# A down projection in 26 products on a 4 x 4 x 2 grid of blocks, where it had 28 from a 2 x 2 x 2 scheme

## The chip, the core and the metric

The kernel runs on one core of a Trainium2 chip. TensorE multiplies matrices from SBUF into PSUM, VectorE and ScalarE work on SBUF and PSUM, GpSimd (POOL in the profile) on SBUF, and SyncE (SP) issues most transfers between SBUF and the chip's memory (DRAM). Each engine takes its instructions in order and waits for others by semaphores. The metric is the device time of one execution in microseconds.

## The reference

A block of a network for 2048 tokens of width 576, all in float32:

```python
xn = layernorm(x)                        # 2048 x 576
s  = linear_attention(xn, wqkv) @ wo     # 32 heads, 2048 x 576
h  = gelu(xn @ w_gate) * (xn @ w_up)     # 2048 x 4608
return x + s * silu(h @ w_down)          # 2048 x 576
```

## The kernel before

**Stages.** The first 300 us make the layer norm, the linear attention and s, which is kept in DRAM (`s_d`). Then come 36 matrices (`matrix`, L713): for each of the 18 groups of 256 columns of F (`g`), one of w_gate and one of w_up. Then comes the down projection (`down_all`, L960).

**Two words.** A float32 operand of TensorE is cut in two fp32r words: the high word is a ScalarE copy, the low word is VectorE's difference (`split`, `cut`). A product of two such operands takes three passes (high x high, high x low, low x high) in down, and seven with the odd rows in gate and up (`PASSES`).

**Gate and up.** Each matrix is a 2 x 2 x 2 product in seven block products after Strassen and Winograd. X's blocks and their sums lie in SBUF as `X`; the weight's sums are formed by GpSimd (`mat_sums`, L666) in one tile, from a raw weight that one transfer brings (`load_mat`, L661). `matrix` runs the seven products one after another, each for two token halves `s` (14 matmuls of 512 columns, in the banks "al", "be", "ga", "de"), and after each one a step of other work from the list `todo[i]`: cutting the next matrix's weight, loading a weight. So a matrix is seven steps, and in this document a step is the time of one of these pieces. The function `done` gets a finished block of the result: for gate it is put through Gelu into a block of `hid`, for up it is multiplied into that block. `hid` are four tiles of two blocks of 128 x 512 each, new in each group.

**Sums of h.** Within an up matrix (`done` in `up_matrix`, L787), GpSimd forms four sums of h for each token half, and SyncE stores the seven forms of h that down wants (`hs_d`). Likewise each group's block of Wd is loaded (`load_down`), turned into four sums on GpSimd (`down_sums`) and stored (`td_d`).

**Down.** Again seven names of products (`PRODUCTS`), each over 18 groups, with two token halves of four token tiles: step `n` is one name and one group, 24 matmuls of 288 columns in eight banks (`down_mm`). The operands come back from DRAM: `load_s` loads h six steps ahead and `prep_s` cuts it three steps ahead into a ring of five; `load_t` loads Wd's form in chunks of four groups eight steps ahead, and `prep_t` cuts it three ahead. At the end of a name's last group, the eight banks are read into sums (`u`, `c22`, `yt`), and finished blocks of the output are closed (`close`): Silu on ScalarE, a product with s on VectorE, a sum with x on GpSimd, and a store. The last name's last four groups run token tile by token tile, so that closing overlaps (`close_last`).

**Order.** The program keeps each engine's order as it is written (`pin`). Tiles with the same tag share a buffer: a new one waits until all users of the old one are done. SBUF is full: 16 large buffers (`big`), three middle ones (`mid`), four `h` slots, six `gl` and four `tmp` tiles pass from stage to stage.

Of the kernel before, what the change touches and what calls it, by code (L numbers as in the profile page):

```python
# [46 lines left out]


# [4 lines left out]
def block_kernel(ctx, tc, x, xe, wq_d, wkv_d, wo, wgu_d, wd_d, out):  # L53
# [659 lines left out]
    def matrix(q, c22, done, todo):  # L713
# [40 lines left out]
    hid = {}  # L754

    def gate_matrix(g, todo):
        for s in SBS:
            for b in range(2):
                hid[s, b] = slot([P, 2, TBN], F32, f"h_{g}_{s}_{b}")

        def done(s, f, b, src):
            o = hid[s, b][:, f]
# [7 lines left out]
        matrix(2 * g, lambda s: hid[s, 1][:, 1], done, todo)  # L770
# [3 lines left out]
    H_AT = {"A11": 0, "A12": 1, "S1": 2, "A22": 3, "S3": 4, "S2": 5, "S4": 6}  # L774
    T_AT = {"T1": 0, "T3": 1, "T4": 2, "T2": 3}
    hs_d = [dr.tile([P, 2, 7, TBN], F32, name=f"hs_{g}") for g in range(NG)]
    td_d = dr.tile([NG, P, 4, HALF], F32, name="td")

    def up_matrix(g, todo):
        c22, sm = {}, {}  # L780
# [6 lines left out]
        def done(s, f, b, src):  # L787
            if src is None:
                src = c22[s]
            elif isinstance(src, tuple):  # L790
                o = src[0] if (f, b) == (1, 0) else tmp([P, TBN], f"u12_{g}_{s}")
                vec("tensor_add", o, *src)
                src = o
            h1, h2 = hid[s, 0], hid[s, 1]
            h = hid[s, b][:, f]
            vec("tensor_mul", h, h, src)
            d = hs_d[g][:, s]
            eng = nc.gpsimd if g == NG - 1 else nc.sync
            if (f, b) == (0, 1):
                sm[s] = [gl_tile([P, TBN], f"hs_{g}_{s}_{i}") for i in range(3)]  # L800
                pool("tensor_sub", sm[s][0], h1[:, 0], h2[:, 0])
                pool("tensor_add", h2[:, 0], h2[:, 0], h2[:, 1])
                pool("tensor_sub", sm[s][1], h2[:, 0], h1[:, 0])
                dma(out=d[:, 4], in_=sm[s][0], eng=eng)
                dma(out=d[:, 2:4], in_=h2, eng=eng)
            elif (f, b) == (1, 0):
                pool("tensor_sub", sm[s][2], h1[:, 1], sm[s][1])
                dma(out=d[:, 0:2], in_=h1, eng=eng)
                dma(out=d[:, 5], in_=sm[s][1], eng=eng)
                dma(out=d[:, 6], in_=sm[s][2], eng=eng)  # L810
# [3 lines left out]
    td = {}  # L814

    def load_down(g):
        td[g] = mid(1, [P, 4, HALF], F32, f"td_{g}")
        dma(out=td[g], in_=wd_d[g].rearrange("p f (c j) -> p (f c) j", c=2))

    def down_sums(g):  # L820

        r = td.pop(g)
        b11, b12, b21, b22 = (r[:, i] for i in range(4))
        pool("tensor_sub", b11, b12, b11)
        pool("tensor_sub", b12, b22, b12)
        pool("tensor_sub", b22, b22, b11)
        pool("tensor_sub", b21, b21, b22)
        dma(out=td_d[g], in_=r)

    PRODUCTS = (  # L830
        ("A11", "B11"), ("A12", "B21"), ("S2", "T2"), ("S1", "T1"),
        ("S4", "B22"), ("S3", "T3"), ("A22", "T4"),
    )
    CHUNKS = ((0, 4), (4, 8), (8, 12), (12, 16), (16, 18))
    T_RAW, T_RING, S_RING = (0, 9, 1), (13, 8, 10), (11, 7, 12, None, None)
    S_FIRST = {3: 3, 4: 5}
    N2 = len(PRODUCTS) * NG
    NC = len(PRODUCTS) * len(CHUNKS)
    tr, hr, tw, hw, made = {}, {}, {}, {}, {"t": 0, "tp": 0, "s": 0, "sp": 0}

    def load_t(upto):

        while made["t"] < min(upto, NC):
            n = made["t"]
            made["t"] += 1
            nm = PRODUCTS[n // len(CHUNKS)][1]
            g0, g1 = CHUNKS[n % len(CHUNKS)]
            r = big(T_RAW[n % len(T_RAW)], [P, 4, HALF], F32, f"tr_{n}")
            if nm in T_AT:
                src = td_d[g0:g1, :, T_AT[nm], :]  # L850
            else:
                f, c = int(nm[1]) - 1, int(nm[2]) - 1
                src = wd_d[g0:g1, :, f, c * HALF : (c + 1) * HALF]
            dma(out=r[:, 0 : g1 - g0], in_=src.rearrange("g p d -> p g d"))
            tr[n] = r

    def cut(hi, lo, src):
        act(hi, src, AF.Copy)
        vec("tensor_sub", lo, src, hi.bitcast(F32))

    def prep_t(upto):
        while made["tp"] < min(upto, NC):
            n = made["tp"]
            made["tp"] += 1
            g0, g1 = CHUNKS[n % len(CHUNKS)]
            o = big(T_RING[n % len(T_RING)], [P, 2, 4, HALF], F32R, f"t_{n}")
# [24 lines left out]
    def prep_s(upto):  # L891
        while made["sp"] < min(upto, N2):
# [3 lines left out]
            if at_:  # L896
                pr = big(at_, [P, 2, 2, TBN], F32R, f"s2_{n}")
# [388 lines left out]
```

## Time and profile before

| | |
|---|---|
| time, median of 3 runs | 1511.56 us (1511.38 to 1512.89) |
| span of the profiled execution, first to last instruction | 1509.8 us |
| first matmul of gate and up | 303 us |
| first matmul of down | 1102.6 us |
| last matmul of down | 1504.3 us |
| bytes moved by DMA | 257.33 MB |

Times in the profile are microseconds from the first instruction, unless marked ns. PE is TensorE's matmuls, PEld its weight loads, DVE VectorE, ACT ScalarE, POOL GpSimd, SP SyncE (SPq: its DMA issues). A group's row reads: line, engine, operation, written tile <- read tiles, shape out <- in, count | busy us, mean ns of one | idle us just before them, and what ended that idle time. A row of the timeline reads: start, length, engine, line, operation, tiles, count [idle before it <- what ended it]. A row of a stretch gives each engine's busy time with its count of instructions, TensorE's granted clock, the busy share of the 16 DMA engines and GB/s.

### The profile page before, as it was taken

The numbers are of one execution on the slowest core, as the hardware profiler recorded it, in microseconds if no ns is written. First come the engines' busy times: TensorE is split into PE (matmuls) and PEld (weight loads), VectorE is DVE, ScalarE is ACT, GpSimd is POOL, SyncE is SP. The second block draws the span as 40 slices with busy tenths as digits, with TensorE's granted clock in tenths as the row PEclk, the third lists the DMA queues.
The fourth block names the chain that finished last, engine by engine and source line by source line (L and its number), as shares of the span: only waits on it lengthen the run. The fifth ranks groups of instructions, "written<-read, shape, count | busy, mean of one in ns | idle before, by whom it ended". The sixth has DMA issues, their size and how long they took to land.

```text
span 1509.8 us, 22224 instructions
## 1 busy us (share of the span) xinstructions
PE 1497.4 (99%) x8344; PEld 1336.7 (89%) x8344; DVE 1068.7 (71%) x1567; ACT 555.4 (37%) x1008; POOL 545.2 (36%) x500
## 2 busy tenths in 40 slices
PE   8999999999999999999999999999999999999998
PEld 7989978988888888888888888888899999999998
DVE  7577466558878777887877788877785566565775
ACT  5434334433222332322223222232336454444443
POOL 4342241135555446555445655544440020000120
PEclk9999999999999999999999999999999999999999
DMA  4525004354433334434333443323678766787873
GB/s 170 181 102 205 5 2 172 141 220 171 160 146 134 116 129 171 171 143 162 110 127 143 171 171 135 151 106 134 213 273 308 236 203 232 240 273 232 295 248 114
DMA packets 112222, 257.33 MB, mean 170 GB/s; under 512 B 10146, under 2 KB 38690, under 8 KB 110066
## 3 DMA queue, kind: packets, MB, share of 16 engines
q1 hardware_dynamic: 110482, 247.00, 45.9%
q0 software_dynamic: 1632, 8.91, 1.6%
q8 instruction: 65, 1.06, 0.3%
q14 instruction: 43, 0.35, 0.1%
HBM read 157.93 MB, written 97.91 MB: 169 GB/s over the span
## 4 chain that ended last, share of the span: by engine, by line
PE 96%; DVE 2%; issue 0%; ACT 0%; DMA 0%; SPq 0%; POOL 0%; DVEq 0%; POOLq 0%; ACTq 0%
PE bd L913 26%; PE al L708 15%; PE de L708 15%; PE ga L708 15%; PE be L708 8%; PE kv L90 7%; PE q L90 4%; PE s L90 4%; PE kv_a L90 1%; PE xt L167 1%; PE d L90 1%; DVE s L87 0%; PE kw L90 0%; PE b L90 0%; DVE xo_B L87 0%
## 5 line engine op out<-in xcount | busy, mean ns | idle before, releaser
L913 PE MATMUL bd<-t,s 128*128 128x288 f32 x3024 | 401.4, 295 | 0.7 <-DVE s L87 0.7
L913 PEld LDWEIGHTS bd<-t,s 128*128 128x128 f32 x3024 | 401.0, 188 | 1.1 <-DVE s L87 0.9
L87 DVE TENSOR_TENSOR s<-sr,s 128x512 fp32r<-128x512 f32 x252 | 182.0, 762 | 117.9 <-ACT s L84 110.9
L84 ACT ACTIVATE s<-sr 128x512 fp32r<-128x512 f32 x252 | 149.0, 626 | 190.9 <-PE bd L913 126.0
L93 POOL TENSOR_TENSOR hs<-h,h 128x512 f32<-128x512 f32 x72 | 100.5, 1404 | 223.8 <-DVE h L87 220.9
L84 ACT ACTIVATE h<-h 128x512 f32<-128x512 f32 x108 | 67.1, 633 | 244.4 <-POOL sm L93 123.1
L93 POOL TENSOR_TENSOR sx<-sx 128x288 f32<-128x288 f32 x24 | 27.9, 1181 | 317.0 <-DVE sx L87 315.9
L90 PE MATMUL kv<-wkv,xo_B 128*128 128x384 f32 x672 | 125.5, 341 | 1.0 <-DVE pk L87 0.3
L90 PEld LDWEIGHTS kv<-wkv,xo_B 128*128 128x128 f32 x672 | 116.8, 189 | 2.7 <-POOL wkv L93 1.1
L87 DVE TENSOR_TENSOR wa<-raw,wa 128x256 fp32r<-128x256 f32 x72 | 80.5, 1119 | 52.1 <-ACT wa L84 46.8
L93 POOL TENSOR_TENSOR sm<-raw 128x384 f32<-128x384 f32 x72 | 75.9, 1054 | 110.4 <-DMA raw<-in_wgu_dram 71.7
L87 DVE TENSOR_TENSOR h<-h,u 128x512 f32<-128x512 f32 x108 | 97.0, 899 | 3.7
L84 ACT ACTIVATE wa<-sm 128x1152 fp32r<-128x1152 f32 x36 | 41.8, 1161 | 134.6 <-PE de L708 134.6
L87 DVE TENSOR_TENSOR wa<-sm,wa 128x768 fp32r<-128x768 f32 x72 | 64.9, 901 | 36.9 <-ACT wa L84 36.1
L93 POOL TENSOR_TENSOR td<-td 128x288 f32<-128x288 f32 x72 | 71.4, 992 | 50.0 <-DMA td<-in_wd_dram 45.8
L87 DVE TENSOR_TENSOR wb<-sm,wb 128x256 fp32r<-128x256 f32 x72 | 61.4, 852 | 20.6 <-ACT wb L84 20.0
L87 DVE TENSOR_TENSOR wb<-raw,wb 128x256 fp32r<-128x256 f32 (+1 forms) x108 | 70.3, 651 | 7.2 <-ACT wb L84 5.6
L84 ACT ACTIVATE u<-al 128x512 f32<-128x512 f32 x72 | 40.9, 593 | 88.3 <-PE al L708 88.3
L90 PE MATMUL q<-xo_B,wq 128*128 128x512 f32 x240 | 64.1, 395 | 0.0
L708 PE MATMUL al<-xo_B,wa 128*128 128x512 f32 x252 | 63.0, 389 | 0.0
L708 PE MATMUL al<-xr_B,wa 128*128 128x512 f32 x252 | 63.0, 389 | 0.0
L708 PE MATMUL be<-xo_T,wa 128*128 128x512 f32 x252 | 63.0, 389 | 0.0
(156 smaller groups left out, 2778.8 us busy)
## 6 DMA issues: line engine op xcount, KB each, us to landing
sr<-hs SPq DMA_DIRECT2D x252, 256.0 KB
hs<-h SPq DMA_DIRECT2D x68, 512.0 KB
raw<-in_wgu_dram SPq DMA_DIRECT2D x36, 768.0 KB
hs<-hs SPq DMA_DIRECT2D x102, 256.0 KB
td<-in_wd_dram SPq DMA_DIRECT2D x18, 576.0 KB
td<-td SPq DMA_DIRECT2D x18, 576.0 KB
tr<-td SPq DMA_DIRECT2D x16, 576.0 KB
tr<-in_wd_dram SPq DMA_DIRECT2D x12, 576.0 KB
```

What stands on the lines that cost most here:

```text
L84: pin(nc.scalar.activation(*args, **kw))
L87: pin(getattr(nc.vector, op)(*args, **kw))
L90: pin(nc.tensor.matmul(*args, **kw))
L93: pin(getattr(nc.gpsimd, op)(*args, **kw))
L167: pin(nc.tensor.transpose(xts[n][j][:, k, :], xs[:, j, k * P : (k + 1) * P], ident))
L708: nc.tensor.matmul(o, w[0:rows, wi, :], xop[0:rows, xi, :], start=(start and n == 0), stop=(n == len(PASSES) - 1), skip_group_check=True,)
L913: nc.tensor.matmul(banks[j][:, 0:HALF], hw[n, s][:, a, t * P : (t + 1) * P], w[:, c, g % 4], start=(new and g == 0 and m == 0), stop=(g == ...
```

## The change

The down projection becomes a product of 4 token blocks by 4 blocks of F by 2 halves of d in 26 block products (`PROD`), each over the nine pairs of groups ("macro blocks", `NM`). A macro block has 16 blocks of h (`var_of`: token block and F block), and 28 sums (`ADDS`: result, two operands, sign, and the step of 28 at which GpSimd forms it). 26 blocks and sums (`FORM`) are stored for down.

*In gate and up.* Blocks and sums of h live in 17 spots: the four `h` slots, the middle buffer 1 that Wd's block had, and the six `gl` tiles. A sum takes the place of an operand that nothing else wants, or the spot that came free first. A sum is formed in its step, stored a step later, and its spot counts as free a step after that. Sums of the last macro block run into down's first products. The results of up are summed in PSUM (into the banks "be", "ga", "de") where they went to SBUF, and multiplied into h from there. Wd's loads, sums and stores are gone from this stage.

*In down.* A product `p` is nine block products (`kt`) in five units (2, 2, 2, 2, 1), each of four token tiles and three passes, in four banks; two sets of banks alternate. The raw blocks of h of a unit are loaded (`load_unit`) once the same unit of the product before is through with its buffer, and cut two units ahead (`cut`); the low word takes the raw block's place. All nine macro blocks of a form of Wd lie in one large buffer (`reg`), eight buffers in all; a form is turned into the next one in place by VectorE (`CHANGES`, done in two halves, for product p + 1 while p runs), loaded anew where needed (`LOADS`, in thirds), and cut into two word buffers (`make_words`, in halves). After its last unit a product's banks are read into one or two of eight output sums (`read`, in the next product's unit 1); a sum's first read is a ScalarE copy, others are VectorE adds or subtractions. A finished output is closed per token tile, in the next product's units 2 to 4, with a store for each tile.

```diff
+ADDS = (
+    (18, 5, 13, 1, 13), (38, 12, 13, 1, 15), (20, 4, 8, -1, 15), (16, 5, 9, -1, 16),
...
+    (42, 17, 37, -1, 34), (29, 2, 10, 1, 34), (26, 10, 17, 1, 36), (30, 20, 26, -1, 36),
+)
+PROD = (
+    (24, 1, 0, ((5, 1), (7, 1))), (18, 1, 0, ((1, 1),)), (14, 0, 1, ((3, 1),)),
...
+    (4, 0, 0, ((4, 1), (6, -1))), (13, 1, 0, ()), (12, 0, 0, ((2, -1),)), (20, 0, 1, ((0, 1),)),
+)
         for s in SBS:
-            vec("tensor_add", c22(s), c22(s), bs["de", s])
-            done(s, 1, 1, None)
+            o = c22(s) if q % 2 == 0 else bs["be", s]
+            vec("tensor_add", o, c22(s), bs["de", s])
+            done(s, 1, 1, o)
...
+    def put_out(m, v, at):
+        eng = nc.gpsimd if m == NM - 1 else nc.sync
+        dma(out=hs_d[m][:, FORM.index(v)], in_=value(m, v), eng=eng)
+        used(m, v, at + 1)
...
+    def add_up(m, v, a, b, sign, at):
+        into = next((x for x in (a, b) if left[m, x] == 1), None)
+        va, vb = value(m, a), value(m, b)
+        born(m, v, None if into is None else place_of[m, into])
+        pool("tensor_add" if sign > 0 else "tensor_sub", value(m, v), va, vb)
...
         def done(s, f, b, src):
-            if src is None:
-                src = c22[s]
-            elif isinstance(src, tuple):
-                o = src[0] if (f, b) == (1, 0) else tmp([P, TBN], f"u12_{g}_{s}")
-                vec("tensor_add", o, *src)
-                src = o
...
+            if isinstance(src, tuple):
+                vec("tensor_add", src[1], *src)
+                src = src[1]
+            v = var_of(g, s, f, b)
+            h = value(m, v)
             vec("tensor_mul", h, h, src)
...
+            if v in FORM:
+                put_later(m, v, 7 * (2 * g + 1) + DONE[f, b])
...
+    UNITS = ((0, 2), (2, 4), (4, 6), (6, 8), (8, 9))
+    REG = {"22": 0, "42": 7, "32": 9, "12": 8, "31": 10, "41": 12, "11": 15, "21": 14}
...
+    def load_unit(p, k):
+        if p >= NP:
+            return
+        raw_v[p, k] = v = raw_place(p, k)
+        for i in range(*UNITS[k]):
+            dma(out=v[:, i - UNITS[k][0]].bitcast(F32), in_=hs_d[i][:, PROD[p][0]])
...
+    def cut(u):
+        p, k = divmod(u, NU)
+        if p >= NP:
+            return
+        hi, lo = hi_place(p, k), raw_v[p, k]
+        hi_v[p, k] = hi
+        src = lo.bitcast(F32)
         act(hi, src, AF.Copy)
         vec("tensor_sub", lo, src, hi.bitcast(F32))
...
+    CHANGES = {
+        4: (("12", "12", "-", "22"),), 5: (("41", "31", "-", "41"), ("32", "41", "+", "32")),
...
+        21: (("21", "21", "-", "32"),), 25: (("11", "11", "-", "31"), ("11", "11", "+", "41")),
+    }
...
+    def change(p, c):
+        for nm, a, op, b in CHANGES.get(p, ()):
+            r = [reg[x][:, HALVES[c]] for x in (nm, a, b)]
+            vec("tensor_add" if op == "+" else "tensor_sub", *r)
...
+    def read(p, js=range(TT)):
+        for o, d in PROD[p][3]:
+            a = acc_of(o)
+            for j in js:
+                src = banks[p % 2][j][:, 0:HALF]
+                if (o, j) not in begun:
+                    begun.add((o, j))
+                    act(a[:, j], src, AF.Copy)
                 else:
...
+                    vec("tensor_add" if d > 0 else "tensor_sub", a[:, j], a[:, j], src)
...
+    def close(o, j):
+        _, cols, rows = places(o)
+        y, t = acc_of(o)[:, j], sxs[o][j]
+        act(y, y, AF.Silu, scale=float(SIGN[o]))
+        vec("tensor_mul", t[:, 0], y, t[:, 0])
+        pool("tensor_add", t[:, 0], t[:, 0], t[:, 1])
+        dma(out=out[rows(j), cols], in_=t[:, 0])
...
+        for u in range(NP * NU):
+            p, k = divmod(u, NU)
+            n = KT * p + 2 * k
+            for at in sorted(events):
+                if at <= H_END + n // 2:
+                    run_events(at)
+            if p in LOADS and k < 3:
+                load_reg(*LOADS[p], k)
+            if k == 0:
+                for o, e in ENDS.items():
+                    if e == p:
+                        load_sx(o)
+            if k < 2:
+                change(p + 1, k)
+            elif k < 4:
+                make_words(p + 1, k - 2)
+            cut(u + 2)
+            if p == last and k == 2:
                 break
...
+            for kt in range(*UNITS[k]):
+                down_mm(p, kt, range(TT))
+            load_unit(p + 1, k)
+            if k == 1 and p:
+                read(p - 1)
+                late += [
+                    lambda o=o, j=j: close(o, j) for o, e in ENDS.items() if e == p - 1
+                    for j in range(TT)
                 ]
+            elif k > 1:
+                run(late, 3)
```

More of the change, by code (lines that the diff above doesn't have):

```diff
@@ new lines, in take_spot, with var_of, value, born @@
+    def take_spot():
+        i = min(free, key=lambda j: (free[j], j))
+        free.pop(i)
+        return i
+    def var_of(g, s, f, b):
+        return TP.index(2 * s + b) * 4 + KP.index(2 * (g % 2) + f)
+    def value(m, v):
+        return spots[place_of[m, v]]
+    def born(m, v, i=None):
+        place_of[m, v] = take_spot() if i is None else i
+        left[m, v] = sum((v == a) + (v == b) for _, a, b, _, _ in ADDS) + FORM.count(v)
+    def used(m, v, at, keep=False):
+        left[m, v] -= 1
+        if left[m, v] == 0 and not keep:
+            free[place_of[m, v]] = at
@@ L768, in done @@
             act(o, src, AF.Gelu_apprx_tanh)
[L770 to L777, printed above, removed]
+        matrix(2 * g, lambda s: h_of(s, 1, 1), done, todo)
     def up_matrix(g, todo):
-        c22, sm = {}, {}
+        c22 = {}
+        m = g // 2
         def take(s):
@@ L812, in up_matrix @@
-        matrix(2 * g + 1, take, done, todo)
[L814 to L850, printed above, removed]
-            else:
[L852 to L855, printed above, removed]
```

351 lines of the change are left out of this document (188 added, 163 removed), and 23 rows, old and new, of tables (ADDS, CHANGES, FROM, LOADS).

## The prediction

> **What bounds the kernel now.** I read the page first, then the chain of waits in order of time, then the stretches.
>
> ```profile
> span 1509.8 us, 22224 instructions
> PE 1497.4 (99%) x8344; PEld 1336.7 (89%) x8344; DVE 1068.7 (71%) x1567; ACT 555.4 (37%) x1008; POOL 545.2 (36%) x500
> PEclk9999999999999999999999999999999999999999
> ```
>
> TensorE is busy for 99% of the span at full granted clock. The chain of waits says the same by stage:
>
> ```profile
> 303.05 3.20 PE al L708 x14
> ...
> 1104.91 4.16 DVE s L87 x2
> 1113.20 391.44 PE bd L913 x2950
> ```
>
> From 303 us on the chain is TensorE alone, but for 4.16 us of VectorE where the down projection begins. So only fewer matmuls can gain, and only a new wait of TensorE can lose. How much room the other engines have is read from stretches of the two stages:
>
> ```profile
> core 0: us, PE busy (x) PEld busy (x) DVE busy (x) ACT busy (x) POOL busy (x), PEclk, DMA share, GB/s
> 700.00:800.00 100.00, 100.00 (x443) 82.78 (x442) 81.23 (x104) 27.29 (x46) 58.33 (x48) 1.00 0.43 158
> ...
> 1135.00:1140.00 5.00, 5.00 (x40) 5.00 (x39) 4.32 (x8) 3.61 (x7) 0.00 (x0) 1.00 1.05 387
> ...
> 1200.00:1300.00 100.00, 100.00 (x757) 100.00 (x756) 62.19 (x88) 49.49 (x80) 9.16 (x8) 1.00 0.67 225
> 1300.00:1400.00 100.00, 100.00 (x757) 100.00 (x756) 57.55 (x88) 47.73 (x79) 5.18 (x5) 1.00 0.72 234
> ```
>
> In gate and up VectorE is 81% busy and GpSimd 58%; in down VectorE is about 60% busy, GpSimd almost idle, and the DMA queues have shown 387 GB/s when full.
>
> **What the change is worth on TensorE.** Before, 7 names x 2 token halves x 18 groups of F are 252 block products (28 nines) of 4 token tiles x 3 passes, 3024 matmuls; now 26 products x 9 macro blocks are 234, 2808 matmuls. The chain gives 391.44 / 2950 = 132.7 ns for each. 216 fewer x 132.7 ns = **-28.7 us**. Shape and passes stay, so the price stays.
>
> **Gate and up: costed at nothing.** Here are the rows.
>
> ```profile
> L93 POOL TENSOR_TENSOR hs<-h,h 128x512 f32<-128x512 f32 x72 | 100.5, 1404 | 223.8 <-DVE h L87 220.9
> L87 DVE TENSOR_TENSOR h<-h,u 128x512 f32<-128x512 f32 x108 | 97.0, 899 | 3.7
> L93 POOL TENSOR_TENSOR td<-td 128x288 f32<-128x288 f32 x72 | 71.4, 992 | 50.0 <-DMA td<-in_wd_dram 45.8
> L87 DVE TENSOR_TENSOR h<-h,al 128x512 f32<-128x512 f32 x36 | 23.2, 685 | 0.5
> ...
> 702.75 1.75 PE L708 MATMUL al<-xo_B,wa 128*128 128x512 f32 x7
> ...
> 723.39 20.17 SPq L96 DMA_DIRECT2D raw<-in_wgu_dram  x2
> ...
> 726.51 1.29 DVE L87 TENSOR_TENSOR h<-u,de 128x512 f32<-128x512 f32 x2
> ```
>
> Per macro block (four matrices, 28 steps of one chain piece, 3.17 us each, 88.8 us) GpSimd did 16 sums of h at 1.40 and 8 of Wd at 0.99; now 28 of h and none of Wd: +16.8 - 7.9 = +8.9 us, from 58% to about 68% busy. VectorE's 108 products h<-h,u now read PSUM and should cost 685 ns like h<-h,al instead of 899: 108 x 0.214 = 23 us less work. An add that writes PSUM has no row; I take the 685 of one that reads it (bounds 685 and 899, 108 of them: 0 to 23 us of VectorE, covered by its 19% idle). Gone too are the loads and stores of Wd's sums on SyncE. Holding the "be" bank until the product with h is no wait: it is wanted by the second product of the next matrix, four products or 12.7 us after the one whose sum it takes.
>
> The tight place is the 17 spots. By the list of sums, the tightest block goes out at step 4, and its spot is rewritten at step 6. Its store stands on SyncE's queue behind the weight load of that step, which waits for its buffer: for the matrix that begins at 702.75 it goes at 723.39, 20.6 us in. The store then lands 2.3 to 4.9 us later (rows below), and VectorE wants the spot at 726.51, 23.8 us in. That is a wait of up to 2 us on VectorE once per macro block, hidden by the PSUM banks: what it delays is wanted three products (9.5 us) later. If that cover is gone, a step is lost per macro block (rival 3).
>
> **The middle of down: VectorE.** Now the prices for the new down stage.
>
> ```profile
> L87 DVE TENSOR_TENSOR xo_T<-xf_B,xo_T 128x1024 fp32r<-128x1024 f32 x8 | 9.8, 1226 | 12.4 <-ACT xo_T L84 12.4
> L87 DVE TENSOR_TENSOR s<-sr,s x37: 677/687/1301, 1200.0 to 1257.8; 128x512 fp32r<-128x512 f32 x37
> L87 DVE TENSOR_TENSOR u_d<-u_d,bd 128x288 f32<-128x288 f32 x15 | 6.4, 454 | 10.2 <-PE bd L913 10.2
> L87 DVE TENSOR_TENSOR sx<-y,sx 128x288 f32<-128x288 f32 x16 | 6.5, 448 | 0.0
> ```
>
> 1024 columns cost 1226 ns and 512 cost 687, so 1.05 ns a column: 1440 columns (five blocks of Wd) 1.66 us, 1152 (four) 1.36, both halves 3.03. A product of 108 matmuls lasts 14.33 us. In it VectorE has: low words of h, 4 x 1.226 + 0.687 = 5.59; low words of Wd, 3.03 (24 of the 26); a change of Wd in place, 3.03 each (20 of them); each read of the four banks into a sum, 4 x 0.454 = 1.82 (23, the first 8 go to ScalarE); four closing products 1.79 (8 outputs). Sum over the stage: 145 + 73 + 61 + 42 + 14 = **335 us of 372.6**, 90%, where it was 60%. The changes of Wd are the new item: GpSimd formed such sums before, in gate and up.
>
> To this comes GpSimd's interference:
>
> ```profile
> 1254.01 1.29 DVE L87 TENSOR_TENSOR s<-sr,s 128x512 fp32r<-128x512 f32 x2 [1.20 <-ACT s L84]
> ...
> 1228.77 2.11 POOL L93 TENSOR_TENSOR sx<-sx 128x288 f32<-128x288 f32 x2 [1.05 <-issue]
> 1228.92 2.50 DVE L87 TENSOR_TENSOR s<-sr,s 128x512 fp32r<-128x512 f32 x2
> ...
> 1104.91 4.16 DVE L87 TENSOR_TENSOR s<-sr,s 128x512 fp32r<-128x512 f32 x2
> 1105.52 1.30 POOL L93 TENSOR_TENSOR hs<-h,h 128x512 f32<-128x512 f32 x1
> 1106.89 1.62 POOL L93 TENSOR_TENSOR h<-h 128x512 f32<-128x512 f32 x1
> ```
>
> Two subtractions take 1.29 us alone and 2.50 beside two 288-wide GpSimd sums: 0.60 per sum. Beside two 512-wide sums they take 4.16: 1.43 per sum. The Trainium skill (SBUF — State Buffer, Who interferes with whom) says that a VectorE instruction with two SBUF inputs contends with GpSimd's reads, and calls the shared port pair "an exclusive lock". By that a 288-wide sum would cost its whole length (2.11 / 2 = 1.05) and not 0.60; the 512-wide rows agree with the rule, the 288-wide do not. By the rule the closings would cost 32 x 0.45 = 14 us more of VectorE, and the sum below would be 1511. I go by the row.
>
> An output's four closing sums thus add 2.4 us. Per product, excess over 14.33: while the 11th runs (15.3 + 2.4) +3.4 and the next (two changes, 16.5) +2.2, together 5.6; the 15th (17.1 + 2.4) +5.2; the 20th and 21st +1.0 and +3.4 = 4.4; the 24th and 25th (15.8 + 4.8; 14.7) +6.3 and +0.4 = 6.7. Lone products with two changes, +2.2, is below the slack. How much can be late unseen? A unit's h is cut two units (6.4 us) ahead; high words, low words and a unit's other work take some 4 of these; 2.5 us of slack remain. It can't grow: the raw buffer is refilled only after its own matmuls, so VectorE can't run ahead in the light products. Stalls: 3.1 + 2.7 + 1.9 + 4.2 = **+12 us**. Bounds: 3, since instructions in a row cost less (1.29 for two, not 1.37, some 40 ns x 370 = 15 us over the stage, about 9 of them where the excess stands); 21, with whole-length sums (4.9 + 4.5 + 3.7 + 7.8).
>
> ScalarE and SyncE stay under this, by these rows:
>
> ```profile
> L84 ACT ACTIVATE s<-sr 128x512 fp32r<-128x512 f32 x252 | 149.0, 626 | 190.9 <-PE bd L913 126.0 <-DMA sr<-hs 49.4 <-DVE sx L87 5.2
> L84 ACT ACTIVATE t<-tr 128x1152 fp32r<-128x1152 f32 x28 | 32.3, 1152 | 3.8 <-DMA tr<-in_wd_dram 3.8
> L96 SPq DMA_DIRECT2D sr<-hs x252: 319/390/1770, 1078.7 to 1477.6; - x126
> SPq L96 <- POOL sx L93: 30.0, 6, 6.7
> ```
>
> ScalarE's high words are 4 x 1.05 + 0.63 + 2.7 = 7.5 us of 14.33, with first reads or closings up to 11. SyncE issues 9 loads of h and up to 15 others at 0.39. Each closing's store now follows its own sum, 32 stores for 8, and waits for GpSimd; three in a row take some 4.5 us, and the loads of h behind them are asked for 12.7 us ahead and need 4.9 to land and 1.9 to be cut: hidden.
>
> **The start of down.** The last macro block's sums fall due after the last matrix.
>
> ```profile
> hs<-hs POOLq DMA_DIRECT2D x6, 256.0 KB, 5.7
> ...
> L96 POOL DMA_DIRECT2D hs<-hs x6: 539/546/584, 1104.4 to 1117.0; - x6
> ...
> DMA to landing us min/median/max: 2.3/4.9/6.6
> ```
>
> GpSimd has 18 sums left there, with stores that it issues itself at 0.55 each; 4.9 us is the median landing. Port: 14 of them fall in the first two products, 14 x 1.43 = 20 us, beside 5.6 + 8.6 us of VectorE and 3 of the last matrix (four adds at 0.69): 37 in 28.7. Of the 8 us over, 2.5 are slack, and GpSimd itself pauses for two landings, so I take 4 late. Order: up to the one that the third product's last unit needs there are 13 sums and 14 stores, 13 x 1.40 + 14 x 0.55 = 26 us, and two sums wait for the landing of a store that frees their spot (4.9 each): 36; that store lands at 41, the unit after it and its cut take 4.9 + 1.9 more, and TensorE wants it at 28.7 + 12.7 = 41.4. That would be 6 late; as part of the landing overlaps, I take 3. SyncE queues that load behind the store, and the next product's loads stand behind it. DMA bytes: the first product has 12 blocks of h to load and 8 to store at 0.26 MB and two forms of Wd at 1.33, 7.9 MB; the second 9, 8 and one, 5.8 MB. At 387 GB/s that is 20.4 and 15.0 us for 14.3 each: 7 us behind, just covered by loads asked for 12.7 us ahead. Together **+7 us** (0, if gaps between sums absorb it, as the 4.16 us before cost TensorE little; to 14, if none overlaps).
>
> **Sum.** 1511.6 - 28.7 + 0 + 12 + 7 = **1502 us**. The profiled execution's span is 1509.8; the runs are 1.8 us longer, and the same is added after: a span near 1500.
>
> **The rivals.** *1: the full gain.* VectorE's excess is absorbed: 3 us in the middle, 0 at the start: 1511.6 - 28.7 + 3 = 1486. For it: runs of instructions are shorter than single ones. Against: 90% of one in-order engine with two units of lead.
>
> *2: VectorE becomes the pace of down.* Whole-length sums (21), 14 at the start, and 1 us for each of four products with two changes, because a change stands ahead of the cuts in the queue: 1511.6 - 28.7 + 21 + 14 + 4 = 1522; it is a loss from the point where these stalls pass 28.7. For it: 335 + 32 x 1.05 = 369 of 372.6. Against: the 0.60 of the rows. The skill's exclusive lock, named above, is this rival's rule.
>
> *3: a spot's wait reaches TensorE in gate and up.* A step of 3.17 us in each of 9 macro blocks is 28.5: 1502 + 28.5 = 1531. For it: a lead of one step. Against: 9.5 us of cover and 19% idle VectorE.
>
> **How the numbers follow.** Forecast 0.50 (1494 to 1514 alone), full gain 0.17, VectorE 0.24, spots 0.09. This measurement can tell 0.2%, 3 us. Faster: all of the full gain and 0.40 of the forecast: 0.57. Within 0.2%: 0.08 of the forecast's upper end and 0.03 of milder forms of rival 2: 0.11. Slower: the rest, 0.32. The range runs from the full gain to about the middle of the two slow rivals, which leaves out less than 0.2: 1485 to 1522.
>
> **What would show it.** After: 2808 matmuls bd at 132.7 ns. VectorE about 90% busy in down, with stalls of 1 to 4 us that end on its cuts of h, near the 11th, 15th and 24th products and in the first three. Gate and up: TensorE 100% busy, no gap. h times up at about 685 ns. It is wrong if gaps stand before al, be, ga or de; if the stalls are ended by DMA; or if VectorE stays under 80% in down.

## The result, and the profile after

The changed kernel takes 1518.61 us (median of 4 runs, 1516.15 to 1521.74), the kernel before 1511.47 beside it: a ratio of 1.0047, 95% interval 1.0033 to 1.0061. It is 7 us slower, where some 10 us less were forecast. The profiled execution, on which all stages and stalls below rest, is the fastest of the four, 1516.15 us; the 2.5 us from there to the median are not in the account.

The page of the changed kernel:

```profile
span 1514.4 us, 21908 instructions
PE 1490.7 (98%) x8128; PEld 1314.1 (87%) x8128; DVE 1151.2 (76%) x1546; ACT 561.1 (37%) x923; POOL 635.9 (42%) x556
PEclk9999999999999999999999999999999999999999
```

TensorE lost only 6.7 us of busy time (1497.4 before), though 216 matmuls, 28.7 us, are gone. So the lost gain is not in gaps alone: part of the matmuls must take longer. Of the span's 4.6 us more, the stages hold (first matmul to first matmul): 1.9 us ahead of gate and up, **+14.3 us in gate and up** (799.7 to 814.0), and -11.5 us from the first matmul of down to the end (407.2 to 395.7). The stretches of gate and up and of down:

```profile
400.00:1100.00 700.00, 699.16 (x3034) 569.18 (x3034) 548.61 (x710) 197.44 (x325) 436.45 (x349) 1.00 0.33 112
1119.00:1508.00 389.00, 377.59 (x2804) 374.70 (x2803) 333.01 (x342) 195.26 (x237) 71.27 (x65) 0.99 0.79 255
```

and the first of them before:

```profile
400.00:1100.00 700.00, 700.00 (x3090) 579.63 (x3089) 550.78 (x726) 204.87 (x340) 365.25 (x310) 1.00 0.41 149
```

In the same 700 us of gate and up TensorE is busy throughout at clock 1.00 in both, and yet makes 3034 matmuls instead of 3090. A busy engine hides this: the count, not the busy share, shows it. Grouped by tiles, before (line, engine, operation, shapes, count, busy us, mean ns):

```profile
L708 PE MATMUL de<-xo_T,wa 128*128 128x512 f32 x224 | 56.0, 389 | 0.0
```

after, in the same stretch:

```profile
L737 PE MATMUL de<-xo_T,wa 128*128 128x512 f32 x217 | 55.6, 395 | 0.0
...
L737 PE MATMUL be<-xr_T,wa 128*128 128x512 f32 x217 | 54.2, 389 | 0.0
```

and TensorE in order of time, after (start, length of the seven matmuls):

```profile
716.04 1.75 PE L737 MATMUL be<-xr_T,wa 128*128 128x512 f32 x7
717.62 1.75 PE L737 MATMUL ga<-xo_T,wa 128*128 128x512 f32 x7
719.21 1.79 PE L737 MATMUL ga<-xr_T,wa 128*128 128x512 f32 x7
720.84 1.79 PE L737 MATMUL de<-xo_T,wa 128*128 128x512 f32 x7
722.47 1.79 PE L737 MATMUL de<-xr_T,wa 128*128 128x512 f32 x7
```

From start to start, the first two groups of seven take 1.58 and 1.59 us, the next ones 1.63: some 233 ns a matmul instead of 226.7. It is not a wait for VectorE, and not the matrix: with the same weights `wa`, in the same product `ga`, one token half is slow and the other is not. What differs between the halves is the buffer in which X lies.

In down the chain of waits shows where TensorE's own pieces are broken off, and what stands there in the longest other pieces:

```profile
1125.27 10.91 DMA raw_a<-hs
1139.70 12.29 PE bd L119 x79
1154.37 106.53 PE bd L119 x802
1261.38 5.31 DMA raw_h<-hs
1299.63 35.01 PE bd L119 x262
1344.15 124.08 PE bd L119 x933
1484.99 23.82 PE bd L119 x166
```

What TensorE waited for directly (us, times, longest us) is VectorE's cuts of h, at the start (`raw_a`) and later (`raw_h`, `raw_g`):

```profile
PE bd L119 <- DVE raw_h L116: 6.9, 5, 3.4
PE bd L119 <- DVE raw_a L116: 4.1, 3, 1.8
...
PE bd L119 <- DVE raw_g L116: 0.2, 1, 0.2
```

From here on a product's stall is the time from its first matmul to the next product's, less 108 times the undisturbed 132.7 ns. Products are counted from 0, as in the code; the prediction counted from 1. The stalls are 4.9 and 2.0 us in products 1 and 2 (the granted clock also fell to 0.89 from 1130 to 1145 us, so not all of the 4.9 is a gap), 2.1 in 11 and 12, 1.6 in 15, 0.1 in 21 and 7.0 in 24: 6.9 at the start and 10.8 later.

**The addresses.** The new tiles of Wd and of its words, `[P, 9, 288]`, have 10368 bytes a partition, the largest tiles of the kernel before, `[P, 5, 512]`, 10240. They share tags with the tiles of the earlier stages, so twelve of the sixteen large buffers grew by 128 bytes and every buffer laid out behind one moved. Before, all operands of gate and up start at a multiple of 256 bytes. After, by the addresses in the built program, `wa` starts at 128 modulo 256, `wb` at 0, and X's blocks thus (token half o, r):

| product | weights | X starts at | operands alike | seven matmuls each |
|---|---|---|---|---|
| al, be (B11, T2) | wa, 128 | 128, 128 | yes, yes | 1.58 to 1.62 us |
| ga (T1) | wa, 128 | 128, 0 | yes, no | 1.59, 1.63 |
| de (T3) | wa, 128 | 0, 0 | no, no | 1.63, 1.63 |
| al (B21) | wb, 0 | 0, 0 | yes, yes | 1.61, 1.59 |
| ga, de (B22, T4) | wb, 0 | 128, 128 | no, no | 1.62 to 1.64 |

Seven of a matrix's fourteen half products are unlike, and the first half product behind one is still a little slow. 7 x 0.045 us and 2 x 0.03 in each of 36 matrices make 13.5 us, near the 14.3. That is so far a fit, and no proof.

### The profile page after: what moved, and what is told of

Its sections match the earlier page's. It is cut to its first block, busy times and chain, and to the rows that moved or that the text cites. A ratio compares the mean times of both kernels' runs of the same rounds, so it can differ in the third digit from the quotient of the medians.

```text
span 1514.4 us, 21908 instructions
## 1 busy us (share of the span) xinstructions
PE 1490.7 (98%) x8128; PEld 1314.1 (87%) x8128; DVE 1151.2 (76%) x1546; ACT 561.1 (37%) x923; POOL 635.9 (42%) x556
## 3 DMA queue, kind: packets, MB, share of 16 engines
q8 instruction: 64, 1.05, 0.3%
## 4 chain that ended last, share of the span: by engine, by line
PE 92%; DVE 4%; DMA 1%; issue 1%; ACT 1%; POOL 0%; SPq 0%; DVEq 0%; ACTq 0%; POOLq 0%
PE bd L119 20%; PE ga L737 15%; PE de L737 15%; PE al L737 15%; PE kv L119 8%; PE be L737 8%; PE q L119 4%; PE s L119 3%; DVE raw_h L116 1%; PE kv_a L119 1%; PE xt L196 1%; DMA raw_a<-hs 1%; PE d L119 1%; DVE sx L116 1%; DVE w L116 0%
## 5 line engine op out<-in xcount | busy, mean ns | idle before, releaser
L119 PE MATMUL bd<-w,hi_m 128*128 128x288 f32 x1568 | 314.2, 295 | 0.0
L119 PEld LDWEIGHTS bd<-w,hi_m 128*128 128x128 f32 x1568 | 252.6, 189 | 0.0
L119 PE MATMUL bd<-w,raw_h 128*128 128x288 f32 x704 | 209.4, 297 | 6.9 <-DVE raw_h L116 6.9
L113 ACT ACTIVATE hi_m<-raw_h 128x1024 fp32r<-128x1024 f32 x88 | 93.2, 1059 | 144.6 <-PE bd L119 110.5
L119 PEld LDWEIGHTS bd<-w,raw_h 128*128 128x128 f32 x704 | 132.7, 188 | 8.6 <-DVE raw_h L116 8.3
L116 DVE TENSOR_TENSOR raw_h<-raw_h,hi_m 128x1024 fp32r<-128x1024 f32 x88 | 110.2, 1267 | 37.1 <-ACT hi_m L113 37.0
L737 PE MATMUL ga<-xo_B,wb 128*128 128x512 f32 x252 | 64.6, 395 | 0.8 <-DVE u L116 0.8
L122 POOL TENSOR_TENSOR spot_h<-spot_h,spot_h 128x512 f32<-128x512 f32 x46 | 63.6, 1390 | 2.9 <-DVE spot_h L116 2.4
L737 PE MATMUL de<-xo_T,wb 128*128 128x512 f32 x252 | 64.7, 395 | 0.0
L737 PE MATMUL de<-xr_T,wa 128*128 128x512 f32 x252 | 64.5, 395 | 0.0
```

Source lines behind the costliest of these rows:

```text
L113: pin(nc.scalar.activation(*args, **kw))
L116: pin(getattr(nc.vector, op)(*args, **kw))
L119: pin(nc.tensor.matmul(*args, **kw))
L122: pin(getattr(nc.gpsimd, op)(*args, **kw))
L737: nc.tensor.matmul(o, w[0:rows, wi, :], xop[0:rows, xi, :], start=(start and n == 0), stop=(n == len(PASSES) - 1), skip_group_check=True,)
```

## The experiments

Times are medians beside runs of the kernel before on the same chip (1511.5 to 1511.9). Gate and up, and the stalls, are each from one profiled execution. The stalls of e1, which has the products of the kernel before, are those of its first 432 matmuls and of the rest; the kernel before has 1.0 there itself.

| kernel | us | ratio to before, interval | gate and up | stalls, products 0 to 3 | later stalls |
|---|---|---|---|---|---|
| changed | 1518.61 | 1.0047 (1.0033 to 1.0061) | 814.0 | 6.9 | 10.8 |
| e1 before, moved | 1525.08 | 1.0089 (1.0072 to 1.0106) | 812.9 | 1.1 | 0 |
| e2 aligned | 1508.36 | 0.9972 (0.9961 to 0.9983) | 801.0 | 8.5 | 16.7 |
| e3 sums in SBUF | 1519.70 | 1.0053 (1.0038 to 1.0068) | 812.9 | 8.4 | 13.1 |
| e4 wb 64 bytes off | 1510.19 | 0.9992 (0.9981 to 1.0003) | 803.7 | 8.6 | 14.1 |
| e11 wb 96 bytes off | 1522.46 | 1.0064 (1.0041 to 1.0086) | 812.4 | 7.5 | 21.0 |
| e5 = e2, loads later | 1506.47 | 0.9962 (0.9948 to 0.9977) | 799.7 | 7.7 | 17.4 |
| e6 = e2, changes earlier | 1499.31 | 0.9917 (0.9902 to 0.9932) | 800.9 | 7.3 | 8.2 |
| e7 = e2, no late sums | 1509.92 | 0.9992 (0.9982 to 1.0001) | 800.4 | 9.8 | 15.7 |
| e13 = e2, stores by GpSimd | 1502.97 | 0.9944 (0.9927 to 0.9960) | 800.4 | 9.0 | 12.2 |
| e8 = e5 + e6, closings spread | 1496.00 | 0.9892 (0.9877 to 0.9906) | 799.8 | 7.3 | 5.7 |
| e10 = e8, no late sums | 1492.01 | 0.9865 (0.9850 to 0.9880) | 800.5 | 2.8 | 6.0 |
| e9 = e8, eight sums on VectorE | 1497.89 | 0.9902 (0.9885 to 0.9918) | 800.5 | 12.4 | 8.7 |
| e12 = e8, block 35 first | 1494.80 | 0.9884 (0.9867 to 0.9900) | 800.6 | 7.6 | 4.7 |
| e14 = e12, stores by GpSimd | **1492.84** | 0.9876 (0.9861 to 0.9890) | 800.6 | 5.8 | 3.8 |

The down stage is the same in the changed kernel, e2, e3, e4 and e11, but for addresses, and yet their stalls are 6.9 to 8.6 us at the start and 10.8 to 21.0 later. So a difference of 2 us at the start, or of several later, between two profiled executions tells nothing by itself; the medians and the traces have to say more.

**Gate and up: e1 to e4, e11.** The theory is the addresses; the rival is that the new work of the other engines slows TensorE. e1 puts the buffer sizes alone into the kernel before; e2 takes the addresses alone back in the changed one, using the 128 bytes that smaller tiles leave free.

```diff
     def big(i, shape, dt, name):
-        return sb.tile(shape, dt, tag=f"b{i}", bufs=1, name=name)
+        if i not in (0, 1, 4, 7, 8, 9, 10, 11, 12, 13, 14, 15):
+            return sb.tile(shape, dt, tag=f"b{i}", bufs=1, name=name)
+        t = sb.tile([P, 2592], dt, tag=f"b{i}", bufs=1, name=name)
+        o = 32 if i in SHIFT and n <= 2560 else 0   # n: floats of shape
+        return t[:, o : o + n]                      # rearranged to shape
# e1: SHIFT = ();  e2: SHIFT = (1, 4, 8, 10, 12, 14)
# e4, e11: as e2, but o = 16 or o = 8 for i == 14, which holds wb
```

> The kernel before; only the sizes of twelve of its sixteen big SBUF buffers are the new ones (10368 instead of 10240 bytes a partition), so that every buffer behind them starts 128 bytes or a multiple later. No instruction is added or left out. Address theory (a 512-wide product takes 3.27 us for fourteen matmuls instead of 3.17 where its two operands don't start alike modulo 256 bytes): gate and up go from 799.7 to about 814 us, the query stage slows too, the time is about 1527. Rival (GpSimd's sums of h, the adds that write PSUM or the spots slow TensorE in gate and up): nothing of these is in this kernel, so 799.7 and 1511.5 stay.

> The changed kernel; in six of the twelve enlarged buffers every tile that leaves room for it starts 128 bytes later, so that all operands of the kv, query, gate and up products start alike modulo 256 bytes again. Instructions are the same. Address theory: gate and up go from 814.0 to about 799.7, the pieces ahead of them lose their 1.85 us more, the down stage keeps its 17.6 us of stalls, the time is about 1502. Rival: 1518.6 and 814 stay.

In e1 gate and up went from 799.7 to 812.9 us and the time up by 13.5; in e2 from 814.0 to 801.0. The same group in e1:

```profile
L723 PE MATMUL de<-xo_T,wa 128*128 128x512 f32 x217 | 55.6, 395 | 0.0
...
L723 PE MATMUL be<-xr_T,wa 128*128 128x512 f32 x219 | 54.8, 389 | 0.0
```

and in e2:

```profile
L752 PE MATMUL de<-xo_T,wa 128*128 128x512 f32 x224 | 56.0, 389 | 0.0
```

No instruction of the change is in e1, and the slow and the undisturbed groups are those of the changed kernel. The rival falls as the cause of gate and up: what the change adds there is worth at most the 1.3 us that e2 keeps (the other aligned versions but e4 and e11 take 799.7 to 800.9). e2's total is 1508, not the expected 1502, since its down stage stalls for 25.2 us instead of the 17.6 that the theory let stand; that is taken up below.

```diff
# e3, on the changed kernel: up's last sums back in SBUF
-            o = c22(s) if q % 2 == 0 else bs["be", s]
-            vec("tensor_add", o, c22(s), bs["de", s])
-            done(s, 1, 1, o)
+            vec("tensor_add", c22(s), c22(s), bs["de", s])
+            done(s, 1, 1, c22(s))
...                                     # and the same in `done` for the other two sums
```

> The changed kernel with up's last sums written to SBUF as before, not to PSUM; addresses as in the changed kernel. Address theory: gate and up stay at 814 us and the time at 1518.6, within 2; VectorE's products with h take 899 instead of some 690 ns. Rival (the adds that write PSUM, or VectorE's and TensorE's meeting in PSUM, slow the matmuls): gate and up go back to about 800, the time to about 1504.

812.9 us and 1519.7: the PSUM writes are not it. The products with h took 772 to 918 ns again.

> As the aligned version of the changed kernel, but the tiles of one buffer, which holds the weights of three of the seven products, start only 64 bytes later: there both operands differ by 64 bytes modulo 128. Tells which part of the address counts. If only the 128-byte bit counts: gate and up at about 800 us, as in the aligned version. If 64 bytes count as much as 128: 3/7 of 3528 matmuls, 1512, at 6.5 ns more, 10 us more, 810. If the rival is right and addresses play no part: 814, as in the changed kernel.

> As the version with one weight buffer 64 bytes off (gate and up 803.7 us, 229 ns a matmul in its three products beside 226.7), but 32 bytes instead of 128 into the buffer, so that the two operands differ by 96 bytes modulo 256. If what counts is the difference modulo 256: between 229 (64 bytes) and 233 (128 bytes), 231 ns and gate and up at 807. If only the 128-byte bit counts, with a small price for any lower bit: 229 again and 803.7.

With `wb` 64 bytes from X (modulo 256) its three products take 229 ns a matmul, with 96 bytes 233.4, about as much as with 128. The groups of e4 and of e11:

```profile
L752 PE MATMUL de<-xo_T,wb 128*128 128x512 f32 x217 | 54.8, 392 | 0.0
```

```profile
L752 PE MATMUL de<-xo_T,wb 128*128 128x512 f32 x217 | 55.8, 396 | 0.0
```

Neither expectation for 96 bytes (231 or 229) was met. So the price doesn't grow evenly with the distance, and it isn't one bit; alike is free, and more is not shown.

**The middle of down: e6 and e13.** The theory is VectorE's excess over a product, as predicted; the rival, SyncE's queue, which the prediction had called hidden. e6 moves five changes of Wd to lighter products:

```diff
-        9: ..., 11: (("12", "11", "+", "12"),),
+        9: ..., 10: (("12", "11", "+", "12"),),
-        15: (("12", "12", "+", "31"),),
+        13: (("12", "12", "+", "31"),),
-        18: (("12", "12", "+", "32"),),
+        18: (("12", "12", "+", "32"), ("21", "21", "-", "32")),
-        21: (("21", "21", "-", "32"),), 25: (("11", "11", "-", "31"), ("11", "11", "+", "41")),
+        22: (("11", "11", "-", "31"),), 23: (("11", "11", "+", "41"),),
```

> The aligned version, with five changes of Wd in place moved to lighter products: that of product 11 to 10, of 15 to 13, of 21 to 18, and the two of 25 to 22 and 23 (a change for product p runs while p - 1 runs). No instruction is added or left out. If VectorE's excess over a product makes the stalls in the middle: those near 11, 15 and 21 go (some 4 to 9 us), those near 24 fall from 7.0 to about 3, where eight closings still stand together; the time falls by 8 to 12 us to about 1498. If they come from GpSimd's slow sums, from SyncE's queue or from loads of h that land late, moving VectorE's work changes little: 1506 to 1508.

1499.3: 9 us less than e2, near the 1498 expected, though not at the places expected. Products 11 and 12 stall for 2.1 us (5.6 in e2), 21 and 22 for 0.1 (2.5), 24 and 25 for 4.4 (7.0); 15 kept its 1.6. The changed kernel's own execution, with none of these changes moved, has the same 2.1 in 11 and 12, 1.6 in 15 and 0.1 in 21. So against it the earlier changes took away only 2.6 us, near product 24, where VectorE had been busy for 25.9 of the 26 us from 1464 to 1490; the stalls of 11, 12 and 15 end on VectorE's cuts as well, but moving changes left them as they were. In e8, which also spreads the closings, that of 15 is 0.6 and those of 11 and 12 are still 2.2.

The rest of the gap to e2, 5.9 us in products 11, 12, 21 and 22, goes with two long GpSimd sums of e2 (6.79 and 5.23 us), which neither e6's execution nor the changed kernel's has. For product 11 of e2, GpSimd, SyncE and ScalarE read, in order of time:

```profile
1266.97 12.60 POOL L137 TENSOR_TENSOR sx<-sx 128x288 f32<-128x288 f32 x4 [115.19 <-DVE sx L131]
```

```profile
1262.88 3.50 SPq L140 DMA_DIRECT2D raw_h<-hs  x3
1273.79 4.26 SPq L140 DMA_DIRECT2D out_dram<-sx  x3
1278.16 0.87 SPq L140 DMA_DIRECT2D raw_h<-hs  x2
```

```profile
1282.17 1.06 ACT L128 ACTIVATE hi_m<-raw_h 128x1024 fp32r<-128x1024 f32 x1 [11.95 <-DMA raw_h<-hs]
```

The first closing sum took 6.79 us alone (0.90 to 0.96 for the first sum of the other closings but one). SyncE stands at its store until 1273.79, the loads of h behind it are asked for at 1278.16, and ScalarE waits for them. e13 has the closings' stores issued by GpSimd:

```diff
         pool("tensor_add", t[:, 0], t[:, 0], t[:, 1])
-        dma(out=out[rows(j), cols], in_=t[:, 0])
+        dma(out=out[rows(j), cols], in_=t[:, 0], eng=nc.gpsimd)
```

> The aligned version; only the stores of the closings are issued by GpSimd itself, right behind its sum, and no longer by SyncE. If SyncE's queue (a store that waits for GpSimd's sum, with the loads of h behind it) makes the stall of product 11: it falls from 5.6 us to the 1.3 or 1.4 of the runs in which the first sum was short, even where that sum takes 6.8 us again, and the time falls by some 4 us to about 1504; the 7.0 us near product 24 stay. If VectorE's excess alone makes it: 5.6 and 1508 stay.

The first sum was as long again, and SyncE went on beside it:

```profile
1265.06 6.79 POOL L137 TENSOR_TENSOR sx<-sx 128x288 f32<-128x288 f32 x1 [114.70 <-DVE sx L131]
```

```profile
1268.23 0.38 SPq L140 DMA_DIRECT2D raw_g<-hs  x1
1268.70 0.38 SPq L140 DMA_DIRECT2D b<-in_wd_dram  x1
1270.99 1.92 SPq L140 DMA_DIRECT2D raw_h<-hs  x2
```

Products 11 and 12 stall for 2.4 us, the time is 1503.0, as expected: a long sum costs little once no load stands behind its store; product 24 got worse (8.8), so the gain there is not all kept.

**The start of down: e5, e7, e8, e10, e12, e9.** The prediction gave VectorE beside GpSimd's late sums ("port") 4 us and the order of sums and stores 3, and DMA bytes nothing. e5 loads four forms of Wd later (12, 21, 31 and 32); e7 leaves the late sums out; e8 takes e5 and e6 and spreads the closings; e10 is e8 without late sums.

```diff
# e5
-        lambda: load_unit(0, 4), lambda: load_reg("32", "32")
+        lambda: load_unit(0, 4)
-        0: ("12", "12"), 1: ("31", "31"), 2: ("21", "21"), 3: ("41", "41"), 4: ("11", "11"),
+        0: ("32", "32"), 1: ("12", "12"), 2: ("31", "31"), 3: ("41", "41"), 4: ("11", "11"),
+        5: ("21", "21"),
# e7, e10
-        pool("tensor_add" if sign > 0 else "tensor_sub", value(m, v), va, vb)
+        if at < HOOKS * NM:
+            pool("tensor_add" if sign > 0 else "tensor_sub", value(m, v), va, vb)
# e8: e5, e6 and
-            elif k > 1:
-                run(late, 3)
+            run(late, 1)
```

> The aligned version of the changed kernel (1508.4 us; stalls of TensorE in its down stage 8.5 us in the first three products, 15.1 later, of them 7.0 near product 24, counted from 0); of the six forms of Wd that are loaded at the end of up and in the first five products, three are loaded one to three products later, one of them (1.33 MB) out of the last matrix. If DMA bytes make the stalls at the start: these fall from 8.5 us to 2 or less and the time to about 1502. If GpSimd's late sums of h make them, by VectorE or by the order of sums and stores, as predicted: 8.5 and 1508 stay, within 2.

> The aligned version without the GpSimd sums of h that fall due after the last matrix; their stores are still made, of what the spot then holds, so the output differs. If these sums make the stalls at the start, by VectorE (4 us predicted) or by their order (3): these fall from 8.5 us to about 1, the time to about 1501. If DMA bytes make them: 6 us or more of them stay, since no byte is left out.

> The aligned version with the later loads of Wd, the earlier changes, and one closing of an output per unit of a product instead of three, so that the eight near product 23 are spread over two products. If both causes are as taken (VectorE's excess in the middle, DMA bytes at the start): stalls of 3 us or less in all, the time about 1486 to 1490, which is the full gain of 28.7 less what the tail holds. If only the middle is settled: about 1494. If neither: 1508.

> The version with later loads, earlier changes and spread closings (1496.0 us; 7.3 us of stalls left in products 2 and 3), without the GpSimd sums of h that fall due after the last matrix (stores kept, so the output differs). If the chain of sums and stores on GpSimd is the second limit at the start, behind the DMA bytes: the 7.3 us fall to 1 or less and the time to about 1489. If something else ends the wait of the loads of h in product 2: 7 and 1496 stay.

Neither alone helps beyond the scatter: e5 keeps 7.7 us, a product later than before, and e7 has 9.8. e8, with e5's and e6's edits, came to 1496.0, nearest to the 1494 expected if only the middle is settled. The stretches say why. In e7, with no late sum, the DMA queues are full over both products:

```profile
1104.00:1120.00 16.00, 15.18 (x112) 14.67 (x110) 10.62 (x11) 3.01 (x4) 12.39 (x17) 1.00 1.07 402
1120.00:1135.00 15.00, 10.45 (x59) 9.46 (x60) 3.03 (x3) 3.79 (x6) 3.25 (x6) 0.85 1.04 407
```

In e5, with fewer bytes, they are not, and TensorE stalls all the same:

```profile
1135.00:1150.00 15.00, 11.37 (x80) 10.42 (x78) 9.78 (x5) 4.00 (x4) 12.51 (x14) 0.98 0.68 230
```

There the load that SyncE asks for at 1140.41, behind the one that ended at 1129.8, is that of the third product's last block, which waits for a store that GpSimd issues at 1133.5, behind a sum that waited 3.93 us for another store to land. With both taken away (e10) the stall is 2.8 us and the time 1492.0, not the 1 us and 1489 expected; the rest stands where the DMA queues are still full (1.05, 406 GB/s from 1120 to 1135 us). So two limits stand one behind the other: DMA bytes first, GpSimd's chain of sums and stores second, and each hides what the other is worth.

```diff
# e12, on e8: the last macro block's late sums begin with
+    LAST_ADDS += [(25, 11, 20, 1, 29), (35, 7, 25, -1, 29)]
# e9, on e8
-        pool("tensor_add" if sign > 0 else "tensor_sub", value(m, v), va, vb)
+        by = vec if HOOKS * NM < at < HOOKS * NM + 5 else pool
+        by("tensor_add" if sign > 0 else "tensor_sub", value(m, v), va, vb)
```

> The same version with all its sums, but of the fourteen late ones the two that lead to the block of h which the third product needs (25 and 35 in the list of sums) are made first instead of eighth and ninth. The count of instructions is the same. If the order of the sums is what is late: the stalls in products 2 and 3 fall from 7.3 us to about 1 and the time to about 1489. If it is the length of GpSimd's work or VectorE's contention with it: 7 and 1496 stay.

> The version with later loads, earlier changes and spread closings (1496.0 us; 7.3 us of stalls in products 2 and 3; 2.8 without the late sums), with the first eight of the fourteen late sums of h on VectorE, at 0.69 us each where GpSimd takes 1.4 and slows VectorE's subtractions beside it from 1.22 to as much as 2.25. The other six stay on GpSimd, since the first of them waits for a store to land. If the late sums' length and their contention are the rest of the start's stalls: GpSimd is done some 15 us earlier, the store of block 35 no longer holds up SyncE, the stalls of products 1 to 3 fall from 7.3 to about 3 and the time to about 1492, as without the sums. If only DMA bytes count there, or VectorE has no room for 5.5 us more: 1496 stays.

e12 took away the wait for block 35 (SyncE asked for it at 1133.56, at 1141.69 in e8), but the time, 1494.8, met neither expectation: the stall came up at another place, 5.8 us in product 2, where VectorE's subtractions stand beside the late sums:

```profile
1134.18 4.60 DVE L131 TENSOR_TENSOR raw_a<-raw_a,hi_a 128x1024 fp32r<-128x1024 f32 x2
1138.70 4.52 DVE L131 TENSOR_TENSOR raw_b<-raw_b,hi_m 128x1024 fp32r<-128x1024 f32 x2
```

That is 2.3 us each for 1.22, and VectorE doesn't pause from 1127.7 to 1152.7 us: this is the part called port. e9, which was to take it away, made the start worse, 12.4 us in the profiled execution (the slowest of its four), and the median 1497.9 where 1492 or 1496 were expected. The sums are shorter on VectorE, but they wait there for stores to land, as GpSimd did, and now the cuts of h stand behind them:

```profile
1113.97 0.69 DVE L131 TENSOR_TENSOR spot_h<-spot_g,spot_h 128x512 f32<-128x512 f32 x1 [4.04 <-DMA hs<-spot_h]
...
1120.66 0.69 DVE L131 TENSOR_TENSOR spot_h<-spot_g,spot_h 128x512 f32<-128x512 f32 x1 [3.06 <-DMA hs<-spot_h]
...
1127.92 0.69 DVE L131 TENSOR_TENSOR spot_g<-spot_m,spot_g 128x512 f32<-128x512 f32 x1 [4.83 <-DMA hs<-spot_g]
```

**The best version: e14**, which is e12 with e13's edit.

> The version with later loads, earlier changes, spread closings and block 35 first (1494.8 us), with the closings' stores issued by GpSimd. Its closings no longer pile up, and its first sums were short: if SyncE's queue counts only where a sum is long, nothing changes (1493 to 1496, stalls of 1.5 and 0.8 us near product 11 stay); if every store on SyncE costs, the stalls of products 11, 12, 15 and 24 (4.0 us in all) fall to about 1 and the time to about 1492.

1492.84 us, 18.7 less than the kernel before. Products 11, 12 and 15 kept their stalls to 0.1 us, 22, 24 and 25 fell (1.8 to 0.9), and the start went from 7.6 to 5.8, which is within the scatter. That is nearer to the first expectation, that SyncE's queue counts only where a sum is long; the total is 2.0 us less than e12's.

## Why the prediction was wrong

**The step that failed is "Gate and up: costed at nothing".** It looked for waits, and found rightly that there would be none: TensorE idled for 0.8 us of 700. It also priced GpSimd's work and each product and sum of VectorE well. But it took the price of a 512-wide matmul as fixed, since no matmul of that stage is edited, and never asked where the larger tiles of down would put the operands of gate and up. Of the 14.3 us that it cost, 13.0 (e2) to 13.2 (e1) come from that. What the 1.9 us ahead of it are is not settled: the aligned versions begin gate and up at 302.4 to 303.9 us, the kernel before at 302.9, the changed one at 304.7. Without this loss the direction was right and the size was not: e2 takes 3.2 us less than the kernel before (0.9961 to 0.9983) where 10 were forecast, since in its profiled execution down stalls for 25 us instead of the 19 forecast.

**What TensorE gains** was right: 2808 matmuls, at 132.5 to 132.6 ns in the undisturbed products.

**Gate and up otherwise.** The products with h took 686 ns (685 forecast), the adds that write PSUM 693. GpSimd rose from 365 to 436 us of 700, as forecast. VectorE's total did not fall with its prices: 549 us of 700 after 551, since the cuts of the weights took longer (768 columns of `wa` 1489 ns on average instead of 1025). That they stand beside more GpSimd sums is the likely reason, not a tested one; it cost TensorE nothing. The spots' wait is there, and hidden, as argued; rival 3 fell:

```profile
DVE spot_h L116 <- DMA hs<-spot_h: 18.4, 6, 4.5
```

**The middle: +12 forecast, 10.8 measured.** The engine was the right one: every one of these stalls ends on VectorE's cuts. The measure, VectorE's excess over a whole product, holds for part of product 24 alone (e6); at 15 the stall stayed with a change less in front of it, and at 11 and 12 it stayed too, where product 11 keeps two changes that the prediction had put below the slack. What within a product makes these is open: the order of VectorE's work there, which no run changed by itself, is a guess. VectorE was busy for 333 us of the stage's stretch (335 forecast), by these rows:

```profile
L116 DVE TENSOR_TENSOR raw_h<-raw_h,hi_m 128x1024 fp32r<-128x1024 f32 x88 | 110.2, 1267 | 37.1 <-ACT hi_m L113 37.0
L116 DVE TENSOR_TENSOR b<-b,b 128x1440 f32<-128x1440 f32 x20 | 35.3, 1766 | 0.1
...
L116 DVE TENSOR_TENSOR sx<-acc,sx 128x288 f32<-128x288 f32 x31 | 18.5, 639 | 0.1
```

The places were those named, though not the sizes: 7.0 us near the 25th product where 4.2 were summed, less at the others, so the near total is partly luck. "Hidden" was wrong for the closings' stores where the first sum is long (e2, e13); in the changed kernel's profiled execution no sum was long, and it held.

**The start: +7 forecast, 6.9 measured**, but by another division. DMA bytes, "just covered", are the first limit, port and order the second (e5, e7, e8, e10). The size was right partly by luck: limits that overlap were added as if they followed each other, with the largest left out.

**Rival 2** has its time nearly right (1522) for a wrong reason: VectorE is not the pace of down (333 us of 389). By the rule it rests on, the Trainium skill's exclusive lock (SBUF — State Buffer, Who interferes with whom), a subtraction would wait for a whole sum; beside 512-wide sums the runs nearly agree (1.22 us became 2.3, beside sums of 1.3). Beside the 288-wide sums of the changed kernel's closings they don't: a cut of 1.21 us took 1.83 (at 1281.4), 0.6 more, as in the prediction's row.

## What to carry to other kernels

When a change enlarges a tile that shares its buffer with tiles of other stages, list the start addresses of all later buffers before and after: matmuls of a stage that the diff never touches can change their price, at full clock and with no gap in the trace. Compare matmul counts in equal stretches and means by tile, not busy shares. Where two limits stand at one place, take both away together before calling either innocent, and ask of every store on a shared queue which loads stand behind it.

## What was not expected of the hardware

A 512-wide matmul follows the last by 226.7 ns where moving and stationary operand start alike modulo 256 bytes, by some 233 where they differ by 128 or 96, by 229 at 64; both at 128 is as good as both at 0. For 288 columns, in down, it is 131.8 for alike and 133.3 for 128 bytes apart (e1). The kernel before has both there: a block of Wd's form has 1152 bytes, so every second block starts 128 bytes off, and the 132.7 of the prediction is the mean of the two prices. Other distances were not tried, and the cause inside the chip is open.

The first GpSimd sum of a closing took 5.2 to 6.8 us in seven of the profiled executions, always at the same two outputs (in e3 at one of them), where a first sum otherwise mostly took 0.8 to 1.0. It was not seen in the six versions with earlier changes, in which VectorE is less pressed, nor in the profiled execution of the changed kernel. So part of what the earlier changes gain over e2 comes with short sums; whether they make the sums short, and what else sets the length, was not tried.

The granted clock was 0.77 to 0.89 in stretches of 15 us with gaps of TensorE at the start of down (0.85 in e7 above); in the changed kernel it was 0.51 for 3.4 us behind a gap, from 1140.7. So a gap costs more than its length.
